# A linear-attention layer and an ELU feed-forward on one core: SP's queue in another order, one block's units three steps apart, and w_out read dense at the end

## The chip, the cores and the metric

One core of one Trainium2 chip. The metric is the device time of one execution in microseconds (us), the median of three runs. The names of the engines are those of the profile: PE is TensorE, DVE VectorE, ACT ScalarE, POOL GpSimd, SP the engine that issues most DMAs.

## The reference

```
# r, k, v: [4, 8, 768, 48]; w, u: [8, 48]; w_in: [384, 2048]; w_out: [2048, 384]
for t in range(768):
    y[t]  = r[t] @ (state + (u * k[t]) outer v[t])       # per batch and head
    state = w * state + k[t] outer v[t]
x = y as [3072 tokens, 8 * 48 channels]
h = x @ w_in
g = where(h > 0, h, exp(min(h, 0)) - 1)
out = g @ w_out                                          # [3072, 384]
```

## The kernel before

**Tiling.** Time is cut into six blocks n of 128 tokens. A block has four **units** (n, b), one for each batch b. A unit computes scores (r by k, decayed), masks them, multiplies them by v, adds what the state gives, and so yields the block's x for its batch; it also adds to the state. A block's x has 4 x 128 = 512 tokens, and the feed-forward runs over it in 16 **steps** f, one for each 128 columns of w_in. The running number of a step is 16 n + f: block 1 starts at step 16, block 2 at 32, block 3 at 48.

**A step.** `hidden` (L1031) writes `ps_h` with nine matmuls: w and x are each split in a high and a low part, and three of the four products are taken for each of three chunks of channels. ACT and DVE make the ELU of it (`negative`, `elu`) and split it in two parts (`split_g`, L1052 and L1054). `project` (L1074) multiplies the split parts of an earlier step by w_out and adds them up in `ps_acc`. Its lag is one step below (n, f) = (1, 4), that is step 20, and two steps from there (`EARLY`). `ps_h` has two buffers. Half of a unit's output, `ps_y`, takes one of them in turn with the steps.

**The last block** (n = 5) is projected by tokens: g is the stationary operand, w_out the moving one, 384 columns wide. w_out lies in the SBUF with its columns permuted (`grouped`, L585), since the other blocks need its columns as rows in that order. So `project` reads it there through `rearrange`, in runs of 32 columns.

**Units from block 2 on.** Their operands are turned through DRAM: DVE transposes r and k in 32 x 32 blocks into `tb` (`t`, `turn_blocks`, L619), SP sends four `blocks` DMAs to DRAM and one back, `rk` (`m`, `move_blocks`, L628 and L633; the latter waits until the four have landed), and POOL multiplies by the powers of w (`br`, `bk`, `decay_moved`, L651). The second of those writes its result back to the buffer of `tb`, and the score matmuls (L758) wait for it. PE's part of a unit stands in `insertion` (`AY`): scores of the new unit, interleaved with the state's part (L766) of the output of the unit before, then that unit's products by v (L791) and the addition to its state (L915).

**x's gap.** A head has 48 channels and 64 rows, so the fourth chunk of an x tile is folded into the free rows of the other three. `G` (`fill_x`, L950) does this with six small DMAs `x<-x` from SP, once the unit's x is split (`xh` on ACT, L940; `xl` on DVE, L942). The first `ps_h` of a block needs the gaps of all its four units.

**What sets the order.** Every engine works in program order, SP's DMA queue too: an issue that waits holds all behind it. The program order is written by hand in two lists of names, `FIRST` for the steps of block 0 and `LATER` for the others. `step` goes through the list once in each step. A name with a letter and a number (`tA-3`, `GY+0`) concerns the unit whose score step (`A`, table `SCORES`) or output step (`Y`, table `OUTPUTS`) is that far from now; a name with a single digit concerns block 1's units in block 0. `rk` and `v` load the raw tensors of a later unit into the slot that this one leaves. There are three slots; the third lies in the tile that held w's raw words (`third_slot`). `ru`, `kr`, `sw`, `p`, `D`, `E` and `sum` are elementwise work of a unit; a `d` behind a name puts it on DVE.

`SCORES` before is 16, 19, 22, 26, 29, 33, 37 and on by fours to 73. Blocks 2 to 5 have four units each, so scores stand at steps 16, 19, 22, 26 (block 2), 29, 33, 37, 41 (block 3), 45 to 57 (block 4), 61 to 73 (block 5). A unit's output is computed in the step of the next unit's scores.

Of the kernel before, what the change touches and what calls it, by code (L numbers as in the profile page):

```python
# [17 lines left out]
P = 128  # L18
B, H, S, D = 4, 8, 768, 48
DP = 64  # L20
HP = H // 2
DM, DFF = 384, 2048
NC = DM // P
# [25 lines left out]


FIRST = """
Eq1 brA-1 rud0 hid ns3 A1 T0 ma sum0 neg mb elu dk0 Y2 xh2 pb1 rk3 tA-3 xl2 sumA-1 sp G2 proj mA-3 gh Lw
Dp0 pa1 lb dr0 r3 gl krd0 swd1 v3 bkA-1 ruA-2 wd r4d third
"""
LATER = """
hid tA-3 AY brA-1 bkA-1 proj neg elu gh gl st nsY+0 xhY+0 xlY+0 paA+1 EqA+1 krA+1 mA-3 rudA-2 pbA+2 swA+2
sumA-1 rkY+0 vY+0 GY+0 DpA+0 out
"""
SCORES = [16, 19, 22, 26] + [13 + 4 * j for j in range(4, 16)]
OUTPUTS = SCORES[1:] + [77]  # L60


class Kernel:
# [319 lines left out]
    def units_at(self, times, step):  # L383
        return [divmod(2 * B + j, B) for j, t in enumerate(times) if t == step]
# [13 lines left out]
    def step(self, n, f):  # L398
        nc = self.nc
# [24 lines left out]
            "Y": lambda n, b: self.outputs(n, b),  # L424
            "xh": lambda n, b: self.split_x(n, b, 0),
            "xl": lambda n, b: self.split_x(n, b, 1),
            "G": lambda n, b: self.fill_x(n, b),
        }
        by_pe = {
            "T": lambda n, b: self.turn_in(n, b),  # L430
# [25 lines left out]
            "lb": lambda: self.low_bits(k + 1),  # L456
            "st": lambda: self.store(last[0]) if last[1] == NF - 1 and last[0] in self.acc else None,
            "out": lambda: self.store_next(),
            "third": lambda: self.third_slot() if (n, f) == (0, 13) else None,
            "AY": lambda: self.insertion(now),  # L460
        }
        now = n * NF + f
        for op in (LATER if n else FIRST).split():
# [3 lines left out]
            if op[-2] in "+-":  # L467
                name, times = op[:-3], (SCORES if op[-3] == "A" else OUTPUTS)
                for m, b in self.units_at(times, now - int(op[-2:])):
# [268 lines left out]
    def insertion(self, now):  # L738

        new, old = (self.units_at(t, now) for t in (SCORES, OUTPUTS))  # L740
        if not new:
# [315 lines left out]
    def project(self, n, f):  # L1057
        gh, gl = self.g.pop((n, f))[2:]
        wh, wl = self.weight(f + 1, 0)
        by_tokens = n + 1 == NCH  # L1060
        if f == 0:
            tags = [(f"acc{c}", 1) for c in range(NC)] + [("rw", 3)] * by_tokens
            self.acc[n] = [
                self.ps.tile([P, 512], F32, tag=tag, name=f"ps_acc{i}", bufs=bufs)
                for i, (tag, bufs) in enumerate(tags)
            ]
        for j, acc in enumerate(self.acc[n]):
            for i, (a, w) in enumerate(((gh, wh), (gh, wl), (gl, wh))):
                if by_tokens:
                    at, lhs = acc[:, 0:DM], a[:, j * P : (j + 1) * P]  # L1070
                    rhs = w.rearrange("p (c i d) -> p i c d", c=NC, i=4)
                else:
                    at, lhs, rhs = acc, w[:, j * P : (j + 1) * P], a
                self.nc.tensor.matmul(  # L1074
                    at, lhsT=lhs, rhs=rhs,
                    start=(f == 0 and i == 0), stop=(f == NF - 1 and i == 2),
                )

    def store(self, n):
        nc = self.nc  # L1080
        acc = self.acc.pop(n)
        if n + 1 == NCH:
            moves = []
            for b, po in enumerate(acc):
                o = self.o.rearrange("p (b d) -> p b d", b=B)[:, b]
                if b % 2:
                    nc.vector.tensor_copy(o, po[:, 0:DM])
                else:
                    nc.scalar.copy(o, po[:, 0:DM])
                row = b * S + n * P  # L1090

                moves.append((self.out[row : row + P, :], o))
                if b != 1:
                    for dst, src in moves:
                        nc.scalar.dma_start(dst, src)
                    moves = []
            return
        o = self.o.rearrange("p (j c d) -> p c j d", j=T // 32, c=NC)
        for c in range(NC):
            nc.vector.transpose(o[:, c], acc[c].rearrange("p (j t) -> p j t", t=32))  # L1100
        self.to_store = [(n, b, i) for b in range(B) for i in range(0, 4, 2)]
        while self.general and self.to_store:
            self.store_next()
# [53 lines left out]
```

## Time and profile before

| | |
|---|---|
| time, median of 3 runs | 530.59 us (529.19 to 530.78) |
| the profiled execution | 528.9 us, its span 527.0 us |
| mean granted TensorE clock | 0.982 |
| PE busy | 503.5 us, 96% |
| DVE, ACT, POOL busy | 59%, 48%, 24% |
| DMA | 50.93 MB, mean 97 GB/s |

The profile is of one execution. Its times count from the start of the span. "Idle before" a row is the time that the engine stood still ahead of it, and the name behind it is what ended that. The granted clock is given as a share of the full 2.4 GHz.

### The profile page before, as it was taken

How to read it: one execution, taken by the hardware profiler on the slowest of the kernel's cores; microseconds unless marked ns; L12 is line 12 of the kernel's file. 1: busy time of each engine (PE TensorE's matmuls, PEld its weight loads, DVE VectorE, ACT ScalarE, POOL GpSimd, SP SyncE). 2: the span in 40 equal slices, each digit the busy share in tenths (PEclk: the TensorE clock that was granted, in tenths of full speed). 3: DMA queues.
4: the chain of work that ended last, by engine and by line, in shares of the span. 5: the costliest groups of instructions: out<-in, count | busy, mean ns of one | idle time of the engine just before them, and what ended most of it. 6: DMA issues, size and time to landing. Idle time of an engine off the chain costs nothing.

```text
span 527.0 us, 9428 instructions
## 1 busy us (share of the span) xinstructions
PE 503.5 (96%) x3584; PEld 416.8 (79%) x3584; DVE 309.1 (59%) x527; ACT 253.5 (48%) x479; POOL 124.6 (24%) x154
## 2 busy tenths in 40 slices
PE   8989999996999999989999989999998999999995
PEld 6987787774878888868888868888786887799995
DVE  5899999983665575645555654654663533433332
ACT  2268788751554345434454453454453543444442
POOL 6832323343231341221311311311202200000000
PEclk9999999997999999999999998999998999999999
DMA  9995869747174444245333344343341200010001
GB/s 136 203 190 136 184 154 232 138 108 155 46 150 108 129 82 107 53 111 124 75 99 94 79 124 90 99 108 77 87 114 38 84 11 8 2 31 24 7 1 65
DMA packets 114203, 50.93 MB, mean 97 GB/s; under 512 B 91362, under 2 KB 110052, under 8 KB 114148
## 3 DMA queue, kind: packets, MB, share of 16 engines
q1 hardware_dynamic: 102052, 45.51, 39.1%
q10 hardware_dynamic: 12096, 4.72, 3.6%
q8 instruction: 30, 0.49, 0.4%
q14 instruction: 25, 0.20, 0.1%
HBM read 35.13 MB, written 13.11 MB: 92 GB/s over the span
## 4 chain that ended last, share of the span: by engine, by line
PE 60%; issue 13%; DMA 8%; DVE 6%; POOL 5%; ACT 4%; SPq 4%; DVEq 0%; POOLq 0%; ACTq 0%
PE ps_acc L1074 25%; PE ps_h L1031 23%; PE ps_y L791 4%; PE ps_a L758 3%; DMA stage<-in_moe_w_in_dram 3%; SPq L950 2%; DMA out_dram<-stage 2%; POOL tb L651 2%; DVE ps_h L1046 1%; PE ps_y L766 1%; PE ps_y L846 1%; ACT g L1041 1%; ACT g L1040 1%; DVE wide L556 1%; POOL a L810 1%
## 5 line engine op out<-in xcount | busy, mean ns | idle before, releaser
L1031 PE MATMUL ps_h<-x,wh 128*128 128x512 f32 (+1 forms) x588 | 181.7, 391 | 4.6 <-DMA x<-x 4.6
L1074 PE MATMUL ps_acc<-g,wh 128*128 128x512 f32 x480 | 166.8, 401 | 0.0
L1046 DVE SCALAR_TENSOR_TENSOR ps_h<-g,ps_h 128x512 f32<-128x512 f32 x96 | 66.6, 694 | 129.3 <-ACT g L1041 129.1
L1031 PEld LDWEIGHTS ps_h<-x,wh 128*128 128x128 f32 x588 | 110.1, 189 | 28.6 <-DMA x<-x 5.0
L1040 ACT ACTIVATE g<-ps_h 128x512 f32<-128x512 f32 x96 | 57.2, 596 | 133.2 <-PE ps_h L1031 121.7
L1031 PE MATMUL ps_h<-x,wl 128*128 128x512 f32 (+1 forms) x294 | 114.4, 389 | 0.0
L1074 PEld LDWEIGHTS ps_acc<-g,wh 128*128 128x128 f32 x480 | 90.6, 189 | 22.0 <-issue 0.9
L1054 DVE TENSOR_TENSOR g<-ps_h,g 128x512 fp32r<-128x512 f32 x96 | 66.3, 691 | 54.2 <-ACT g L1052 52.2
L1074 PE MATMUL ps_acc<-g,wl 128*128 128x512 f32 x240 | 94.3, 393 | 0.0
L1052 ACT CAST g<-ps_h 128x512 fp32r<-128x512 f32 x96 | 56.3, 587 | 65.9 <-DVE ps_h L1046 65.3
L1031 PEld LDWEIGHTS ps_h<-x,wl 128*128 128x128 f32 x294 | 55.7, 189 | 12.0
L1041 ACT ACTIVATE g<-g 128x512 f32<-128x512 f32 x96 | 60.7, 632 | 3.0
L651 POOL TENSOR_TENSOR stage<-rk,pw 128x512 f32<-128x512 f32 x16 | 19.0, 1186 | 170.4 <-DMA rk<-blocks 160.9
L1074 PEld LDWEIGHTS ps_acc<-g,wl 128*128 128x128 f32 x240 | 45.5, 190 | 9.0
L1074 PE MATMUL ps_acc<-wh,g 128*128 128x384 f32 x128 | 35.3, 339 | 0.0
L810 POOL TENSOR_TENSOR a<-ident,diag 128x512 f32<-128x512 f32 x20 | 20.9, 1043 | 56.8 <-PE ps_y L791 53.5
L758 PE MATMUL ps_a<-stage,tb 48*64 48x128 f32 x512 | 26.0, 284 | 7.3 <-POOL tb L651 6.3
L758 PEld LDWEIGHTS ps_a<-stage,tb 48*64 48x64 f32 x512 | 21.5, 139 | 14.0 <-POOL tb L651 10.4
L940 ACT CAST x<-ps_y 128x256 fp32r<-128x256 f32 x40 | 13.1, 377 | 33.6 <-DVE state L930 21.1
L817 DVE COPY_PREDICATED a<-mask,ps_a 128x512 f32<-128x512 int32 x40 | 28.9, 730 | 0.0
L806 ACT ACTIVATE a<-ident,diag 128x128 f32<-128x128 f32 x80 | 25.6, 396 | 0.0
L1074 PEld LDWEIGHTS ps_acc<-wh,g 128*128 128x128 f32 x128 | 23.4, 188 | 1.1 <-issue 0.4
(127 smaller groups left out, 513.6 us busy)
## 6 DMA issues: line engine op xcount, KB each, us to landing
blocks<-tb SPq DMA_DIRECT2D x64, 128.0 KB, 2.3
rk<-blocks SPq DMA_DIRECT2D x16, 512.0 KB, 3.5
stage<-in_moe_w_out_dram SPq DMA_DIRECT2D x16, 384.0 KB, 5.0
stage<-in_moe_w_in_dram SPq DMA_DIRECT2D x32, 144.0 KB, 4.3
out_dram<-stage ACTq DMA_DIRECT2D x80, 48.0 KB, 1.7
r_t<-in_r_dram SPq DMA_DIRECT2D x17, 192.0 KB, 4.3
k_t<-in_k_dram SPq DMA_DIRECT2D x17, 192.0 KB, 4.2
v_t<-in_v_dram SPq DMA_DIRECT2D x17, 192.0 KB, 3.7
```

The source lines that it names most:

```text
L651: self.nc.gpsimd.tensor_mul(dst, src, by)
L758: nc.tensor.matmul(un["pa"][i][keys, a * P : (a + 1) * P], lhsT=un["k"][rows, a, keys], rhs=un["r"][rows, a, :], start=True, stop=True, sk ...
L806: self.nc.scalar.activation(un["a"][i][:, a, :], self.ident, AF.Copy, scale=diag[:, a : a + 1])
L810: self.nc.gpsimd.tensor_mul(un["a"][i], self.ident.unsqueeze(1).to_broadcast([P, HP, P]), diag.unsqueeze(2).to_broadcast([P, HP, P]),)
L817: self.nc.vector.copy_predicated(un["a"][i], self.mask.bitcast(I32).unsqueeze(1).to_broadcast([P, HP, P]), un["pa"][i].rearrange("p (a t) ...
L1031: self.nc.tensor.matmul(ph[:, part], lhsT=a[:, c * P : (c + 1) * P], rhs=x[:, c, part], start=(c == 0 and i == 0), stop=(c == NC - 1 and i ...
L1040: nc.scalar.activation(g, ph, AF.Relu, scale=-1.0)
L1041: nc.scalar.activation(g, g, AF.Exp, scale=-1.0)
L1046: self.nc.vector.scalar_tensor_tensor(ph, g, -1.0, ph, op0=ALU.add, op1=ALU.max)
L1052: nc.scalar.copy(part, g)
L1054: nc.vector.tensor_sub(part, g, self.g[n, f][2].bitcast(F32))
L1074: self.nc.tensor.matmul(at, lhsT=lhs, rhs=rhs, start=(f == 0 and i == 0), stop=(f == NF - 1 and i == 2),)
```

## The change

```
-Eq1 brA-1 rud0 hid ns3 A1 T0 ma sum0 neg mb elu dk0 Y2 xh2 pb1 rk3 tA-3 xl2 sumA-1 sp G2 proj mA-3 gh Lw
-Dp0 pa1 lb dr0 r3 gl krd0 swd1 v3 bkA-1 ruA-2 wd r4d third
+Eq1 rud0 hid ns3 A1 T0 ma sum0 neg mb elu dk0 Y2 xh2 pb1 rk3 xl2 tA-3 sp G2 proj mA-3 gh Lw
+Dp0 pa1 lb dr0 r3 gl krd0 swd1 v3 rudA-2 wd r4d third

-hid tA-3 AY brA-1 bkA-1 proj neg elu gh gl st nsY+0 xhY+0 xlY+0 paA+1 EqA+1 krA+1 mA-3 rudA-2 pbA+2 swA+2
-sumA-1 rkY+0 vY+0 GY+0 DpA+0 out
+hid AY tA-3 brA-1 bkA-1 proj neg elu gh gl st nsY+0 xhY+0 xlY+0 paA+1 EqA+1 krA+1 pbA+2 mA-3 rudA-2 swA+2
+sumA-1 rkY+0 vY+0 GlY+0 GY+1 DpA+0 out

-SCORES = [16, 19, 22, 26] + [13 + 4 * j for j in range(4, 16)]
+SCORES = [17, 20, 23, 26] + [13 + 4 * j for j in range(4, 16)]

-            "G": lambda n, b: self.fill_x(n, b),
+            "G": lambda n, b: self.fill_x(n, b) if n == 1 or b < B - 1 else None,
+            "Gl": lambda n, b: self.fill_x(n, b) if b == B - 1 else None,

-            "third": lambda: self.third_slot() if (n, f) == (0, 13) else None,
+            "third": lambda: self.third_slot() if (n, f) == (0, 14) else None,

 # project, last block
-                    at, lhs = acc[:, 0:DM], a[:, j * P : (j + 1) * P]
-                    rhs = w.rearrange("p (c i d) -> p i c d", c=NC, i=4)
+                    at, lhs, rhs = acc[:, 0:DM], a[:, j * P : (j + 1) * P], w

 # store, last block
-                if b % 2:
-                    nc.vector.tensor_copy(o, po[:, 0:DM])
-                else:
-                    nc.scalar.copy(o, po[:, 0:DM])
+                po = po[:, 0:DM].rearrange("p (c i d) -> p i c d", c=NC, i=4)
+                (nc.vector.tensor_copy if b % 2 else nc.scalar.copy)(
+                    o.rearrange("p (i c d) -> p i c d", c=NC, i=4), po
+                )
```

In `store`, the copies that empty the last block's sums now read the PSUM in the order i, c, d and write their tile in one run. Everything from L428 on stands one line lower in the changed kernel, up to `project`.

The first three units of block 2 have their scores at steps 17, 20 and 23; with them move their transposes, DMAs and elementwise work, the loads of the third slot (one step later), and the outputs, since `OUTPUTS` is made of `SCORES`. The gap of a block's first three units is issued one step later, behind the `blocks` and the `rk` of a unit that comes two later; a block's last unit keeps its place (`Gl`).

**SP's queue around the end of block 0.** `blocks` and `rk` are those of unit (2, 0), `stage` the third slot, `x<-x` the gap of unit (1, 3). Before:

```order
L169 DMA v_t_70<-in_v_dram 128x8x48
L628 DMA blocks<-tb 32x4x256 x4
L633 DMA rk<-blocks 128x1024
L165 DMA stage<-in_r_dram 128x8x48
L165 DMA stage<-in_k_dram 128x8x48
L169 DMA stage<-in_v_dram 128x8x48
L950 DMA x<-x 16x2x128 x6
```

Now:

```order
L169 DMA v_t_70<-in_v_dram 128x8x48
L951 DMA x<-x 16x2x128 x6
L629 DMA blocks<-tb 32x4x256 x4
L634 DMA rk<-blocks 128x1024
L165 DMA stage<-in_r_dram 128x8x48
L165 DMA stage<-in_k_dram 128x8x48
L169 DMA stage<-in_v_dram 128x8x48
```

The gap has passed from behind the blocks, their return and the third slot's three loads to ahead of them.

**SP's queue in steps 33 and 34.** The loads and the gap belong to the unit whose output is computed at step 33, `blocks` and `rk` to the unit whose scores stand at step 37. Before:

```order
L165 DMA stage<-in_r_dram 128x8x48
L165 DMA stage<-in_k_dram 128x8x48
L169 DMA stage<-in_v_dram 128x8x48
L950 DMA x<-x 16x2x128 x6
L628 DMA blocks<-tb 32x4x256 x4
L633 DMA rk<-blocks 128x1024
```

Now:

```order
L165 DMA stage<-in_r_dram 128x8x48
L165 DMA stage<-in_k_dram 128x8x48
L169 DMA stage<-in_v_dram 128x8x48
L629 DMA blocks<-tb 32x4x256 x4
L634 DMA rk<-blocks 128x1024
L951 DMA x<-x 16x2x128 x6
```

The four blocks and their return stand ahead of the gap. The same holds at steps 49 and 65, and for the other units of a block but its last.

**PE behind the first insertion that has an output.** Before, at step 19, where `ps_acc` follows:

```order
L791 MATMUL ps_y<-a,v_t_70 64x128 x8
L915 MATMUL ps_y<-v_t_70,k_t_69 48x48 x8
L1074 MATMUL ps_acc_1581<-g_1637,wh_133 128x512
L1074 MATMUL ps_acc_1581<-g_1637,wl_134 128x512
L1074 MATMUL ps_acc_1581<-g_1639,wh_133 128x512
```

Now, at step 20, where `ps_h` of the next step follows:

```order
L792 MATMUL ps_y<-a,v_t_70 64x128 x8
L916 MATMUL ps_y<-v_t_70,k_t_69 48x48 x8
L1032 MATMUL ps_h<-x,wh_137 128x512 x2
L1032 MATMUL ps_h<-x,wl_138 128x512
L1032 MATMUL ps_h<-x,wh_137 128x512 x2
```

The insertion has moved into the step that has no `project`.

## Rows read from the trace of the kernel before

**Rows 1.** The page: PE's and its weight loads' busy time with the other engines' (section 1), and the granted clock in 40 slices of 13.2 us, in tenths (section 2).

```profile
PE 503.5 (96%) x3584; PEld 416.8 (79%) x3584; DVE 309.1 (59%) x527; ACT 253.5 (48%) x479; POOL 124.6 (24%) x154
...
PEclk9999999997999999999999998999998999999999
```

**Rows 2.** The waits of PE: line and tile, what ended the wait, us in total, times, longest us.

```profile
PE ps_a L758 <- POOL tb L651: 6.3, 6, 2.2
PE ps_h L1031 <- DMA x<-x: 4.6, 1, 4.6
```

**Rows 3.** PE's timeline: start us, duration us, engine, line, operation, output and inputs, count, and in brackets the idle time before and what ended it. The rows with long idle time outside the start, and the insertion of step 19 with the `ps_acc` behind it.

```profile
110.88 1.09 PE L791 MATMUL ps_y<-a,v_t 128*64 128x128 f32 x16 [0.49 <-DVE a L817]
...
123.31 1.19 PE L1031 MATMUL ps_h<-x,wh 128*128 128x512 f32 x2 [4.58 <-DMA x<-x]
...
141.90 0.33 PE L758 MATMUL ps_a<-stage,tb 48*64 48x128 f32 x2
...
144.75 0.50 PE L1074 MATMUL ps_acc<-g,wh 128*128 128x512 f32 x1
...
157.03 0.55 PE L758 MATMUL ps_a<-stage,tb 48*64 48x128 f32 x10 [0.90 <-DVE a L817]
...
233.35 0.33 PE L758 MATMUL ps_a<-stage,tb 48*64 48x128 f32 x2 [2.15 <-POOL tb L651]
...
315.70 0.33 PE L758 MATMUL ps_a<-stage,tb 48*64 48x128 f32 x2 [1.96 <-POOL tb L651]
...
397.62 0.33 PE L758 MATMUL ps_a<-stage,tb 48*64 48x128 f32 x2 [1.64 <-POOL tb L651]
```

**Rows 4.** Windows: the stretch, its length, busy us (and count) of PE, PE's weight loads, DVE, ACT and POOL, the granted clock, the DMA share, GB/s. Directly behind the 4.58 us, and 1.7 us behind the end of the 2.15 us.

```profile
123.30:125.30 2.00, 1.99 (x5) 1.63 (x6) 0.00 (x0) 0.00 (x0) 0.02 (x1) 0.50 0.68 134
...
235.00:237.40 2.40, 2.40 (x33) 2.31 (x31) 0.00 (x0) 0.00 (x0) 0.55 (x1) 0.50 0.02 7
```

**Rows 5.** The chain of waits, pieces in order of time: start us, us, what. Steps 16 and 17, step 33, step 37.

```profile
123.31 4.18 PE ps_h L1031 x9
127.50 1.83 PE ps_a L758 x32
...
131.60 2.08 PE ps_h L1031 x9
...
211.52 0.33 PE ps_a L758 x2
...
212.19 0.44 PE ps_a L758 x16
...
216.73 2.05 PE ps_h L1031 x9
...
233.35 0.33 PE ps_a L758 x2
...
240.13 2.08 PE ps_h L1031 x9
```

**Rows 6.** SP's timeline (columns as in rows 3): the gap and the blocks for step 37, the blocks for steps 53 and 69.

```profile
219.36 3.78 SPq L950 DMA_DIRECT2D x<-x  x6
223.23 1.97 SPq L628 DMA_DIRECT2D blocks<-tb  x4
...
305.75 1.97 SPq L628 DMA_DIRECT2D blocks<-tb  x4
...
386.78 1.98 SPq L628 DMA_DIRECT2D blocks<-tb  x4
```

**Rows 7.** DVE's timeline: the last transposes ahead of those blocks.

```profile
219.87 0.67 DVE L619 STREAM_TRANSPOSE tb<-k_t 128x512 f32<-128x512 f32 x1
...
301.76 1.30 DVE L619 STREAM_TRANSPOSE tb<-stage 128x512 f32<-128x512 f32 x2
...
383.42 0.67 DVE L619 STREAM_TRANSPOSE tb<-k_t 128x512 f32<-128x512 f32 x1
```

**Rows 8.** SP's timeline in steps 13 to 16: unit (2, 0)'s blocks and return, the gap of unit (1, 3).

```profile
110.24 1.77 SPq L628 DMA_DIRECT2D blocks<-tb  x4
115.39 0.34 SPq L633 DMA_DIRECT2D rk<-blocks  x1
...
118.66 4.03 SPq L950 DMA_DIRECT2D x<-x  x6
```

**Rows 9.** DVE's timeline: the split of unit (1, 3)'s x, the ELU of step 15, and the last use of `ps_h` at step 19.

```profile
113.70 0.75 DVE L942 TENSOR_TENSOR x<-ps_y,x 128x256 fp32r<-128x256 f32 x2
...
118.00 0.70 DVE L1046 SCALAR_TENSOR_TENSOR ps_h<-g,ps_h 128x512 f32<-128x512 f32 x1 [2.24 <-ACT g L1041]
...
144.72 0.69 DVE L1054 TENSOR_TENSOR g<-ps_h,g 128x512 fp32r<-128x512 f32 x1 [0.65 <-ACT g L1052]
```

**Rows 10.** POOL's timeline: the product that ends unit (2, 0)'s round trip.

```profile
120.11 1.26 POOL L651 TENSOR_TENSOR tb<-rk,qw 128x512 f32<-128x512 f32 x1
```

**Rows 11.** DMA issues by target and source: queue, count, KB each, median us from issue to landing. The third slot's loads of r.

```profile
stage<-in_r_dram SPq DMA_DIRECT2D x5, 192.0 KB, 4.1
```

**Rows 12.** The chain of waits near the end: nine matmuls of 512 columns (block 4) and twelve of 384 (block 5).

```profile
456.19 2.08 PE ps_acc L1074 x9
...
464.83 2.10 PE ps_acc L1074 x12
```

## The prediction

> **What bounds the kernel now.** I read the page first: PE is busy 503.5 us of a 527.0 us span and the granted clock is full in nearly every slice [rows 1]. So what can be won is PE's idle time and the slow clock behind it, and little else. The waits of PE, taken by themselves, name two large causes: the score matmuls waiting for POOL's `tb`, 6.3 us in six waits, and one `ps_h` matmul waiting 4.6 us for the DMA `x<-x` [rows 2]. PE's timeline gives the places [rows 3]: 2.15, 1.96 and 1.64 us at 233, 316 and 398 us, which are the scores of steps 37, 53 and 69, the second score step of blocks 3, 4 and 5; 4.58 us at 123 us, the first `ps_h` of block 1 (step 16); 0.90 us at 157 us (step 22); 0.49 us at 111 us (step 14). The windows show what follows a long one: PE had run without a gap, stood for about 2 us, and some 1.7 us after it resumed the granted clock is 0.50, the 1.2 GHz level; after the 4.58 us it is 0.50 at once [rows 4]. The chain of waits prices that [rows 5]. From the first score matmul of a unit to the next `ps_h` it takes 5.21 us at step 33 (211.52 to 216.73) and 6.78 us at step 37 (233.35 to 240.13): the slow clock costs 1.57 us more. After the 4.58 us, nine `ps_h` matmuls take 4.18 instead of 2.08 us and 32 score matmuls 1.83 us, where 16 take 0.44 at the full clock: 2.10 + 0.95 = 3.05 us.
>
> Why is `tb` late at steps 37, 53 and 69? SP's queue shows it: six issues of x's gap take 3.8 us, and only then do the next unit's four `blocks` leave, at 223.23, 305.75 and 386.78 [rows 6]. The transposes that feed those blocks had ended 2.69 us earlier each time, at 220.54, 303.06 and 384.09 [rows 7]. From a unit's first block to its scores the round trip is 10.12, 9.95 and 10.84 us (233.35, 315.70, 397.62 less the three starts). In those steps DVE first turns the finished block's sums, so x is split late, the gap waits for it at the head of SP's queue, and the blocks wait behind.
>
> **The change part by part.** *x's gap behind the next unit's blocks.* For a block's second unit the four blocks and `rk` now stand ahead of the gap, so they leave 2.69 us earlier, when the transposes end. That is more than each wait: 0.54, 0.73 and 1.05 us are left over. What goes: 2.15 + 1.96 + 1.64 = 5.75 us idle and 3 x 1.57 = 4.71 us of slow clock, **10.46 us**. The gap now lands some 5 us later; nothing reads it before the next block's first `ps_h`, several steps on, and for a block's last unit, where that is near, it stays ahead. If one of the three waits stayed, 3.5 us of this would be lost.
>
> *The handover to block 1 (steps 13 to 17).* Before, SP issues unit (2,0)'s blocks at 110.24, its `rk` at 115.39, then three loads for the third slot, and only at 118.66 the gap of unit (1,3), for which PE waits [rows 8]. The gap's input was ready when DVE had split it, at 114.45 [rows 9]. Now the gap goes first. The two transposes (1.3 us) also leave DVE's queue ahead of the last score mask and of the split, so the 0.49 us goes and the split ends near 113.35. The six issues take 4.03 us, to 117.4, and PE resumed 0.62 us after the last one (122.69 to 123.31), so x is there at 118.05. PE, which ran dry at 123.31 - 4.58 = 118.73, now does so at 118.24. The wait of step 16 goes, and its slow clock with it.
>
> But unit (2,0)'s blocks now leave at 117.4, not 110.24. Its own round trip was 11.13 us (110.24 to the end of `tb` at 120.11 + 1.26) [rows 10], so its scores can start at 128.5. They are due one step later than before, at 118.24 + 2.08 (`ps_h`) + 2.08 (`ps_acc`) + 2.08 (`ps_h`) = 124.5. **What is late next is therefore this unit**: about 4.0 us idle at step 17. With the shortest trip, 9.95, it is 2.85 us. The slow clock behind it lies between 1.57 us (after about 2 us) and 3.05 us (after 4.58 us); I take 3.05, as 4.0 is nearer to 4.58.
>
> The three loads of the third slot move with it, behind `rk`, to about 123; a load lands 4.1 us after its issue [rows 11], at 127.3, before the transposes of (2,1) at 128.5, which wait for POOL anyway. Two products of (2,0) pass from POOL to DVE (1.1 us) and fall into DVE's idle 2.24 us before 118.00 [rows 9]. I cost both at nothing. If the loads were 2 us later, the transposes and the ELU behind them would be late, but the hidden block's product is not needed until some 6 us after the scores.
>
> *Block 2 three steps apart.* The scores move from steps 16, 19, 22 to 17, 20, 23. Step 20 is the one in which no `ps_acc` is issued (the lag grows from one step to two there). Before, two `ps_h` stood side by side there, DVE fell behind by a step's work, and the mask that the scores of step 22 need came 0.90 us late; now the scores of step 20 stand between the two, and I let the 0.90 us go. But `ps_h` of step 21 follows those scores directly. It needs the `ps_h` buffer that DVE has yet to read. At step 19 DVE ended that read 3.5 us after the scores began (141.90 to 144.72 + 0.69) and PE's insertion took 2.85 us (to 144.75) [rows 3, 9]: a new wait of 0.6 us; between nothing, if DVE is early, and 0.9.
>
> Handover and block 2 together: gone 4.58 + 3.05 + 0.49 + 0.90 = 9.02 us; new 4.0 + 3.05 + 0.6 = 7.65 us; **1.4 us gained**. At the short trip and the small clock cost it would be 9.02 - 2.85 - 1.57 - 0.6 = 4.0; with a trip 1 us longer than (2,0)'s own, 0.3.
>
> *Dense w_out.* The 192 matmuls of the last block read w in one run instead of runs of 32. In the chain twelve of 384 columns take 2.10 us, 175 ns each; nine of 512 dense columns take 2.08, 231 ns each, and three quarters of that is 173 [rows 12]. So runs of 32 cost at most 1.7 ns: 192 x 1.7 = **0.3 us**. The last copy reads PSUM in runs of 32 instead; I put that at nothing, at most 0.3 us, which would cancel the gain. The Trainium skill ("TensorE: Matmul & The Clock Gate", section "Wait — 56ns, not 53.3ns?") has back-to-back matmuls start N / 2.4 GHz + about 2.5 ns apart, 162.5 ns for 384 columns; by that the reordered read would cost 12.5 ns each, 2.4 us in all, and the sum would be 2.1 us lower. The dense rows of this trace stand at 231 ns, where the page would have 215.7, so the excess is not the read order's.
>
> Sum: 10.46 + 1.4 + 0.3 = 12.2 us. The profiled execution took 528.9 us, so 516.7. The three runs before lie at 529.19 to 530.78, median 530.59, all above it; I forecast the new median at **517.5 us**.
>
> **The rivals.** *The handover pays nothing or loses* (0.15). If DVE does not split x earlier (114.45 stays), the gap lands at 119.1, PE waits 0.4 us at step 16, the blocks leave 1.1 us later and step 17 idles some 5 us with the full slow clock: 1.4 turns into about -1.5. For it: ACT's part of the split waits for PE too. Against: DVE's queue loses the 1.3 us. Time 520.5.
>
> *The gap now flies beside `rk`* (0.12). Issued right behind `rk`, its six transfers share the engines with it, and the 0.54 to 1.05 us are used up. Waits of 0.5 to 1 us at two or three places would return 1.5 to 3 us, without a slow clock (after the 0.90 us at 157 us the slices of [rows 1] stay full). Against: the gap moves 16 KB an issue. Time 519.5.
>
> *The round trip is bound by transfers, and the kernel gets slower* (0.05). Blocks sent at once meet the finished block's output stores, which ACT issues in those very steps. With a trip c the four places idle c - 10.6, c - 10.6, c - 11.9 and c - 7.1; together with the new 0.6 us this equals what goes (5.75 + 4.58 + 0.90 + 0.49 + 0.3) at c = 12.9, from which it decides. At c = 14 it is 3.4 + 3.4 + 2.1 + 6.9 us, slow clock as before, 4.4 us slower: 533. For it: 10.84 and 11.13 are above the other two. Against: no trip in the trace reaches 11.2. The Trainium skill ("DMA: Bandwidth & Descriptors", section "Issuing engines are not separate DMA queues") says that transfers of all issuing engines run on the same 16 DMA engines and interleave; by that rule the trips should lengthen, and the trace shows a spread of 1.2 us at most.
>
> *Dense reads are worth 12.5 ns* (0.06): another 2.1 us, 515.4.
>
> That the change doesn't do what it says, the order of the issues excludes for the places that I count; only a block's last unit keeps its gap in front, and no large wait stands there.
>
> **How the numbers follow.** My forecast has 0.62. The range 512.5 to 522.5 takes in the other three cases that are faster and the far ends of the handover (4.0 and 0.3) and of one wait that stays; it leaves out the slow case and mishaps of several kinds. No change means within 0.3%, 1.6 us, about what a measurement of this kernel can tell. Faster 0.93: all cases but the slow one and a little of others; same 0.02; slower 0.05.
>
> **What would show it.** Right: PE's timeline has no wait over 0.5 us at the scores of steps 37, 53 and 69, and the clock stays at 1.00 behind them; in SP's queue `blocks` start as the transposes end, with trips of 10 to 11 us; step 16 starts without a wait; one wait of 2.8 to 4 us for `tb` at step 17, with 0.50 behind it; about 0.6 us before `ps_h` of step 21; twelve `ps_acc` in 2.08 us at the end. Wrong: trips over 12 us, a wait for `x<-x`, or `ps_acc` of the last block under 170 ns.

## The result, and the profile after

The changed kernel takes **516.42 us**, the median of four runs (515.16 to 517.58), where the kernel before took 529.89 us (528.90 to 530.78) beside it: a ratio of 0.9746, 95% interval 0.9714 to 0.9777, or 11.8 to 15.2 us less. The forecast was 517.5 us in a range of 512.5 to 522.5. The profiled execution is the one of 517.58 us, the longest of the four; the profiled one of before, 528.9 us, was its shortest.

The page of the changed kernel, first its span, then the rows that answer to [rows 1]:

```profile
span 515.8 us, 9426 instructions
...
PE 498.1 (97%) x3584; PEld 412.5 (80%) x3584; DVE 316.7 (61%) x529; ACT 253.5 (49%) x479; POOL 125.0 (24%) x152
...
PEclk9999999999899999999999999999999999999999
```

PE is busy 5.4 us less for the same 3584 matmuls. Less of its time runs at the low clock: where [rows 1] has three lower slices, one is left. DVE is busy 7.6 us more. Its products of `ru` alone take 31.8 us where they took 22.2; two of the 40 have moved to DVE (1.1 us), and the rest is that eleven of them take 1.08 to 1.54 us instead of 0.55 (before, two took 0.76 and 1.53). e8 is about that.

The waits of PE, as [rows 2]: line and tile, what ended the wait, us in total, times, longest.

```profile
PE ps_a L759 <- POOL tb L652: 3.8, 3, 3.0
PE ps_a L733 <- DVE rk L664: 3.6, 4, 1.5
...
PE ps_h L1032 <- DVE g L1055: 1.0, 1, 1.0
PE ps_a L759 <- DVE a L818: 0.8, 2, 0.5
```

And its timeline, as [rows 3], the idle time from step 13 on where it is over 0.25 us:

```profile
106.41 1.16 PE L733 MATMUL ps_a<-rk 48*128 48x128 f32 x16 [1.54 <-DVE rk L664]
...
129.60 1.60 PE L759 MATMUL ps_a<-stage,tb 48*64 48x128 f32 x32 [3.03 <-POOL tb L652]
...
149.41 0.73 PE L1032 MATMUL ps_h<-x,wh 128*128 128x512 f32 x2 [1.01 <-DVE g L1055]
...
192.35 0.54 PE L759 MATMUL ps_a<-stage,tb 48*64 48x128 f32 x10 [0.54 <-DVE a L818]
...
290.56 0.33 PE L759 MATMUL ps_a<-stage,tb 48*64 48x128 f32 x2 [0.51 <-POOL tb L652]
...
369.41 0.33 PE L759 MATMUL ps_a<-stage,tb 48*64 48x128 f32 x2 [0.30 <-POOL tb L652]
```

Nothing stands at the scores of steps 37, 53 and 69, nothing at step 16 and nothing at step 23 (the mask that was late at step 22). What is left: 1.54 us for DVE's `rk` at step 13 (no such wait before; the last paragraph of the account comes back to it), 3.03 us at step 17, 1.01 us at the `ps_h` of step 21, 0.54 us at step 29 (new), 0.51 and 0.30 us at steps 49 and 65 (0.20 us each before).

SP's timeline, as [rows 6, 8]: the handover first, then the blocks for steps 37, 53 and 69.

```profile
115.65 3.80 SPq L951 DMA_DIRECT2D x<-x  x6
119.54 1.97 SPq L629 DMA_DIRECT2D blocks<-tb  x4
...
220.58 1.78 SPq L629 DMA_DIRECT2D blocks<-tb  x4
...
299.62 1.79 SPq L629 DMA_DIRECT2D blocks<-tb  x4
...
376.90 1.78 SPq L629 DMA_DIRECT2D blocks<-tb  x4
```

DVE's timeline, as [rows 7, 9]: x's split of unit (1, 3), the last transpose for step 37, and two products of step 27.

```profile
114.88 0.75 DVE L943 TENSOR_TENSOR x<-ps_y,x 128x256 fp32r<-128x256 f32 x2
...
186.63 1.51 DVE L695 TENSOR_TENSOR ru<-stage,u_b 128x384 f32<-128x384 f32 x1
188.18 1.53 DVE L696 TENSOR_TENSOR ru<-ru,stage 128x384 f32<-128x384 f32 x1
...
219.88 0.67 DVE L620 STREAM_TRANSPOSE tb<-k_t 128x512 f32<-128x512 f32 x1
```

POOL's, as [rows 10]: the end of unit (2, 0)'s trip, and what it does beside DVE's two products.

```profile
128.28 1.26 POOL L652 TENSOR_TENSOR tb<-rk,qw 128x512 f32<-128x512 f32 x1
...
186.54 1.19 POOL L652 TENSOR_TENSOR stage<-rk,pw 128x512 f32<-128x512 f32 x1 [6.39 <-DMA rk<-blocks]
187.68 1.61 POOL L652 TENSOR_TENSOR tb<-rk,qw 128x512 f32<-128x512 f32 x1
```

The blocks for step 37 leave at 220.58, 0.03 us after the transposes that end at 220.55. From first block to the end of `tb` the trips at steps 37, 53 and 69 take 10.0, 10.4 and 11.0 us. The handover's gap goes out at 115.65, as DVE's split ends (115.63), and the blocks of (2, 0) at 119.54; their trip ends at 129.54, after 10.0 us.

The chain of waits, as [rows 5, 12]: what follows the 3.03 us, and one projection of the last block.

```profile
129.60 1.60 PE ps_a L759 x32
131.21 3.34 PE ps_acc L1074 x9
134.54 2.08 PE ps_h L1032 x9
...
454.36 2.09 PE ps_acc L1074 x12
```

To compare kernels by stage I take the time from the first `ps_h` of one step to that of a later one, from PE's timeline of each profiled execution (us):

| steps | before | changed | e1 gap | e2 handover | e3 dense | e4 junk |
|---|---|---|---|---|---|---|
| 13 to 24 (handover, block 2) | 63.86 | 62.36 | 64.32 | 60.08 | 64.77 | 65.12 |
| 36 to 39 (scores of 37) | 19.30 | 15.50 | 15.50 | 17.73 | 19.30 | 17.72 |
| 52 to 55 (scores of 53) | 19.04 | 15.46 | 15.46 | 17.73 | 20.90 | 17.87 |
| 68 to 71 (scores of 69) | 18.38 | 15.14 | 15.15 | 18.32 | 16.75 | 16.49 |
| 81 to 95 (last block) | 58.78 | 58.46 | 58.79 | 58.79 | 58.46 | 58.77 |

Between the two executions profiled first, the three stretches of the gap give 3.80 + 3.58 + 3.24 = 10.62 us and the last block 0.3; steps 13 to 24 give 1.50, and steps 24 to 36, which the change also touches (step 29), cost 0.79. The row of steps 13 to 24 has to be read with step 13 in mind: the executions of the changed kernel and of e4 have a wait of about 1.5 us there, the other four of the table under 0.4 us.

### The profile page after: what moved, and what is told of

Same layout as the page of the kernel before. It is cut to its first block, busy times and chain, and to the rows that moved or that the text cites. A ratio compares the mean times of both kernels' runs of the same rounds, so it can differ in the third digit from the quotient of the medians.

```text
span 515.8 us, 9426 instructions
## 1 busy us (share of the span) xinstructions
PE 498.1 (97%) x3584; PEld 412.5 (80%) x3584; DVE 316.7 (61%) x529; ACT 253.5 (49%) x479; POOL 125.0 (24%) x152
## 4 chain that ended last, share of the span: by engine, by line
PE 71%; DVE 8%; issue 6%; DMA 5%; ACT 5%; POOL 3%; SPq 1%; DVEq 0%; ACTq 0%; POOLq 0%
PE ps_acc L1074 31%; PE ps_h L1032 29%; DMA stage<-in_moe_w_in_dram 5%; PE ps_y L792 3%; PE ps_a L759 3%; DVE ps_h L1047 2%; DVE wide L557 1%; ACT stage L549 1%; PE ps_y L767 1%; DVE wide L565 1%; PE ps_y L847 1%; ACT stage L543 1%; PE ps_y L916 1%; ACT g L1041 1%; POOL tb L652 1%
## 5 line engine op out<-in xcount | busy, mean ns | idle before, releaser
L1032 PEld LDWEIGHTS ps_h<-x,wl 128*128 128x128 f32 x294 | 55.2, 188 | 11.9
```

The source lines that it names most:

```text
L1032: self.nc.tensor.matmul(ph[:, part], lhsT=a[:, c * P : (c + 1) * P], rhs=x[:, c, part], start=(c == 0 and i == 0), stop=(c == NC - 1 and i ...
```

## The experiments

e1 to e3 are the kernel before with one part of the change each, and e4 is the kernel before with a few matmuls added. e5 to e8 alter one thing in the changed kernel, c1 to c4 build on e8. Ratios are to the kernel before, run beside them; differences in us from the kernel before are worked out from the ratio, those from the changed kernel are differences of medians.

**e1: the gap alone.** The kernel before with

```
-sumA-1 rkY+0 vY+0 GY+0 DpA+0 out
+sumA-1 rkY+0 vY+0 GlY+0 GY+1 DpA+0 out
```

and the two entries for `G` and `Gl`.

> The kernel before with x's gap behind the next unit's blocks for a block's first three units, and nothing else of the change. My theory: the waits of 2.15, 1.96 and 1.64 us at the scores of steps 37, 53 and 69 go and the clock stays full behind them, 10.46 us in all, so 10.5 us below the kernel before; the 4.58 us at step 16 and the 0.90 us at step 22 stay. Rival (the gap flies beside rk): waits of 0.5 to 1 us stay at two or three of these places, 7.5 to 9 us gained. Rival (the three waits cost only their idle time, and the slow clock behind them would come anyway): 5.75 us gained.

Measured: 519.6 us, ratio 0.9827 (0.9779 to 0.9875), 9.2 us less (6.6 to 11.7). In the trace the three waits are gone (the table: 15.50, 15.46 and 15.15 us, those of the whole change) and the handover is the old one. PE's timeline, the first `ps_h` of block 1, and the only other wait for `tb` over 0.3 us:

```profile
124.34 1.19 PE L1032 MATMUL ps_h<-x,wh 128*128 128x512 f32 x2 [4.57 <-DMA x<-x]
...
292.44 0.33 PE L759 MATMUL ps_a<-stage,tb 48*64 48x128 f32 x2 [0.75 <-POOL tb L652]
```

The mechanism is shown. The gap flying beside `rk` used no margin up, so that rival falls, and the 5.75 us of the other lie outside the interval. Whether the slow clock was priced rightly, e2 and e4 tell.

**e2: the handover and block 2 alone.** The new `FIRST`, `tA-3` behind `AY`, `pbA+2` ahead of `mA-3`, the new `SCORES`, the third slot at (0, 14); `GY+0` and the reads of w_out as before.

> The kernel before with the new order of steps 12 to 15, block 2's scores at steps 17, 20 and 23 and the third slot one step later; the gap keeps its place behind later units' outputs, w_out is read as before. My theory, by the prediction's terms: 1.4 us gained. By what the changed kernel's trace shows of the terms (3.03 us idle at step 17 with about 1.7 us of slow clock, 1.01 and 0.23 us at steps 21 and 20, against 9.02 us that go): about 3 us gained. Rival (the handover loses): 1.5 us slower. The waits at steps 37, 53 and 69 stay, about 2 us each.

Measured: 525.65 us, ratio 0.9911 (0.9872 to 0.9950), 4.7 us less (2.6 to 6.8). The part that I had put at 1.4 us is worth more. PE's timeline, the scores of steps 17 and 37:

```profile
128.04 1.10 PE L758 MATMUL ps_a<-stage,tb 48*64 48x128 f32 x32 [3.04 <-POOL tb L651]
...
229.76 0.33 PE L758 MATMUL ps_a<-stage,tb 48*64 48x128 f32 x2 [2.15 <-POOL tb L651]
```

The wait at step 37 is 2.15 us, as in [rows 3]. But the chain shows the products by v and the `ps_acc` behind it at the full clock, and those behind the 1.60 us of step 69 at the low one:

```profile
231.31 1.02 PE ps_y L791 x16
232.69 2.30 PE ps_acc L1074 x9
...
392.98 1.90 PE ps_y L791 x16
394.88 2.82 PE ps_acc L1074 x9
```

Behind the same 2.15 us the kernel before had a granted clock of 0.50 [rows 4]; here the window behind it has 1.00:

```profile
231.50:233.90 2.40, 2.40 (x38) 2.11 (x35) 0.71 (x2) 0.24 (x1) 1.45 (x2) 1.00 0.03 8
```

The stretch takes 17.73 us in place of 19.30: 1.57 less, with the wait still there. Step 53 repeats it (2.15 us of wait, 17.73 us). Steps 13 to 24 take 3.78 us less than before in this execution.

**e3: w_out read dense, alone.** `rhs` is `w` in the last block, and the last copies permute.

> The kernel before with the last block's w_out read in one run of 384 columns, and the permuted copies at the end. My theory: 0.3 us gained, at most 0.4 (a step of the last block takes 4.155 us instead of 4.18 in the changed kernel's chain, sixteen times), which the runs can hardly tell from nothing. Rival (reads in runs of 32 cost 12.5 ns a matmul): 2.4 us gained.

Measured: 530.37 us, ratio 1.0004 (0.9974 to 1.0034), between 1.4 us less and 1.8 us more. The runs exclude 2.4 us and can't see 0.3. The trace can: steps 81 to 95 take 58.46 us where all kernels with the old read take 58.77 to 58.79, so 0.32 us for fourteen steps and 0.37 for sixteen, 1.9 ns a matmul.

**e4: the slow clock behind the three waits.** The kernel before with

```
+        for _ in range(6 if now in (37, 53, 69) else 0):
+            nc.tensor.matmul(un["pa"][0][:, 0:P], lhsT=self.ident, rhs=self.ident, start=True, stop=True)
```

in `insertion`.

> The kernel before with six more 128 x 128 matmuls (about 0.235 us each, 1.41 us in all, their result is overwritten) on PE ahead of the scores of steps 37, 53 and 69. They fill part of the 2.15, 1.96 and 1.64 us that PE waits for tb, and end no wait. My theory: PE goes on in these places at the full clock, the 3 x 1.57 us behind the waits go, 4.7 us below the kernel before, while the scores start at the same distance from their blocks; idle of about 0.7, 0.5 and 0.2 us is left. Rival (the slow stretch has another cause than the idle PE): no gain, the clock still 0.50 behind the scores. Second rival (the junk is in the way): up to 1 us slower.

Measured: 527.38 us, ratio 0.9965 (0.9929 to 1.0002), 1.9 us less (3.8 less to 0.1 more). PE's timeline and the chain behind it:

```profile
235.81 0.33 PE L762 MATMUL ps_a<-stage,tb 48*64 48x128 f32 x2 [0.79 <-POOL tb L651]
```

```profile
237.36 1.02 PE ps_y L795 x16
238.74 2.30 PE ps_acc L1078 x9
```

In the profiled executions the three stretches are 1.58, 1.17 and 1.89 us shorter than before, 4.64 together, as the theory had it. The runs give under half of that, and their interval leaves 4.7 out. The theory's price holds where the low clock comes, but it does not come behind every such wait in every execution: e2 shows that at step 37, and so does e3 at step 69, with 1.53 us of wait and 16.75 us for the stretch, where the kernel before had 1.64 us [rows 3] and 18.38. The clocks of the runs agree. 29 runs of the kernel before had a mean granted clock of 0.978 to 0.993. Span x (1 - clock), an estimate of what the low clock costs a run, is 3.7 to 11.7 us there, 8.0 on average; in the ten runs of e4 it is 5.3. That is 2.6 us for the three places, not 4.7.

The second rival, that the junk is in the way, is not excluded by this. In e4's profiled execution steps 39 to 52 take 64.97 us where the kernel before had 63.25, with waits of 0.92 and 0.87 us for `tb` at steps 45 and 49, and no run tells whether the extra matmuls had a part in that. The estimate from the clock does not depend on it.

**e5: the step without `ps_acc` one later.** The changed kernel with `EARLY = (1, 5)`.

> The changed kernel with EARLY = (1, 5) in place of (1, 4): the step without ps_acc is 21 instead of 20, so nine ps_acc (2.08 us) stand between the insertion of step 20 and the ps_h of step 21. My theory (that ps_h waits because it follows the insertion directly): the 1.01 us at step 21 goes, no wait over 0.3 us takes its place, 1.0 us gained on the changed kernel's 516.42. Rival (the wait is the gap between DVE's work and PE's over the whole stretch, and moves with it): a wait of about 1 us appears at the next place, the scores or the ps_h of step 23, and the time is the same.

Measured: 518.64 us, ratio 0.9776 (0.9711 to 0.9841). The 1.01 us is gone, and PE's timeline has this at step 23:

```profile
160.64 0.55 PE L759 MATMUL ps_a<-stage,tb 48*64 48x128 f32 x10 [2.03 <-DVE a L818]
```

The rival holds in its mechanism: DVE is behind over the whole stretch, and the wait moves to where its work is next needed. It does not hold in size, since 2.03 us are twice what went; c2 takes that apart. The median is 2.2 us above the changed kernel's, with overlapping intervals, and the profiled execution lost more to the clock behind the 2.85 us at its step 17. The chain there:

```profile
127.93 1.98 PE ps_a L759 x32
129.92 4.14 PE ps_acc L1074 x9
```

**e6: the slow clock at step 17.** The same extra matmuls as in e4, `11 if now == 17 else 0`, in the changed kernel.

> The changed kernel with eleven more 128 x 128 matmuls (0.235 us each, 2.6 us in all, their result is overwritten) on PE ahead of the scores of step 17, in the 3.03 us that PE waits for tb. My theory: about 0.4 us of idle time is left, the clock stays full behind it, nine ps_h take 2.08 instead of 3.34 us and the 32 score matmuls under 1.2 instead of 1.60 us: 1.7 us gained in an execution that had the slow clock there. Rival (no slow clock is saved, or the junk pushes the scores later in executions whose wait is shorter): no change.

Measured: 514.68 us (514.46 to 515.64), ratio 0.9713 (0.9666 to 0.9760). The expected 1.7 us below the changed kernel's median; the two intervals overlap, so the size rests on the trace and the clock. PE's timeline:

```profile
127.86 1.10 PE L763 MATMUL ps_a<-stage,tb 48*64 48x128 f32 x32 [0.58 <-POOL tb L652]
```

And the chain behind it:

```profile
128.96 2.28 PE ps_acc L1078 x9
```

The 32 score matmuls take 1.10 instead of 1.60 us and the nine `ps_acc` behind them 2.28 instead of 3.34, so the low clock behind the 3.03 us had cost 0.50 + 1.06 = 1.56 us. The mean clock of the four runs is 0.998, of the changed kernel's 0.995. The expectation named `ps_h` where `ps_acc` stands.

**e7: the last unit's gap behind the blocks too.** `GY+1` for all four units in the changed kernel.

> The changed kernel with the gap of a block's last unit behind the next blocks too (GY+1 for all four units). My theory: the 0.51 and 0.30 us at the scores of steps 49 and 65 go, and no wait for x<-x appears at the first ps_h of steps 32, 48, 64 and 80, since the last unit's output is computed three steps ahead: 0.8 us gained. Rival (that gap is needed soon, which its own place in the change would suggest): waits for x<-x at two or more of those steps, slower.

Measured: 520.61 us, ratio 0.9804 (0.9751 to 0.9858). The rival holds: PE waits 1.41, 2.25 and 1.14 us for `x<-x` at the first `ps_h` of steps 32, 48 and 64. The longest of the three, and SP's timeline ahead of step 32:

```profile
286.90 0.70 PE L1031 MATMUL ps_h<-x,wh 128*128 128x512 f32 x2 [2.25 <-DMA x<-x]
```

```profile
197.64 1.77 SPq L628 DMA_DIRECT2D blocks<-tb  x4
201.31 0.34 SPq L633 DMA_DIRECT2D rk<-blocks  x1
201.75 3.79 SPq L950 DMA_DIRECT2D x<-x  x6
```

`rk` holds the queue from 199.4 until the blocks have landed, and only then do six issues follow, to 205.54; PE needed x at 204.55 (205.96 less 1.41). Behind the blocks and `rk`, the gap starts 4.1 us after the first block (201.75 less 197.64). Here that is too late.

**e8: DVE's products away from POOL's.** In the changed kernel `rudA-2` stands behind `AY` instead of behind `mA-3`, so the two products of `ru` come ahead of that step's ELU.

> The changed kernel with the two products of ru (two steps ahead of a unit's scores) at the start of that step's work on DVE, ahead of the ELU, where DVE stands idle 2.85 us at 181.20, instead of at its end, where they run beside POOL's two products. My theory (DVE's and POOL's products slow each other): every ru product takes 0.55 to 0.56 us where the changed kernel's took up to 1.55, the 0.54 us at step 29 and the 0.23 us at step 20 go, and part of the 1.01 us at step 21: 0.8 to 1.3 us gained. Rival (the long ones are something else, as data that is still landing): they stay at 1.5 us and the waits stay.

Measured: 514.90 us, ratio 0.9723 (0.9673 to 0.9773), 1.5 us below the changed kernel's median, again with overlapping intervals. DVE's timeline, the products of step 27:

```profile
177.35 0.55 DVE L695 TENSOR_TENSOR ru<-stage,u_b 128x384 f32<-128x384 f32 x1
177.94 0.56 DVE L696 TENSOR_TENSOR ru<-ru,stage 128x384 f32<-128x384 f32 x1
```

The same two products took 1.51 and 1.53 us beside POOL's in the changed kernel, so the theory holds and the rival falls. All means of `ru`'s groups on DVE are 547 to 559 ns now, the 0.54 us at step 29 and the 0.23 us at step 20 are gone, and the wait at step 21 is 0.65 instead of 1.01 us. Steps 24 to 36 take 58.83 us, where the changed kernel had 59.83 and the kernel before 59.04.

Moving the products also takes 1.1 us of work from that place in DVE's order, so e8 alone does not show that their slowness made the waits. Other executions do, with the products in the old place. Ahead of the scores of step 20 they took 1.08 and 1.54 us in the changed kernel and 0.94 and 1.53 in e7, and PE waits 1.01 us at step 21 in both. In e2 and e6 they end as POOL starts or before, and take 0.54 and 0.56 us; there step 20 waits for nothing, and step 21 waits 0.66 us. Ahead of the scores of step 29 it is the same: 0.54 us of waiting behind products of 1.51 and 1.53 us, 0.30 behind 1.26 and 1.53 (e6), and none behind 1.10 and 0.76 (e2).

**c1: the handover's gap from two queues.** e8, and of unit (1, 3)'s gap the half i = 1 is issued by `nc.scalar` behind `gh` (a `Ga2` in `FIRST`).

> The changed kernel with ru early (as in e8_ru_early, 514.9 us) and with three of the six issues of unit (1, 3)'s gap on ACT's queue, behind split_g, where ACT stands idle 3.13 us ahead of the ELU at 116.23. My theory (the 2.75 us at step 17 are unit (2, 0)'s round trip, which starts only when SP has issued the gap): the blocks of (2, 0) start about 1.9 us earlier, 0.8 us of the wait is left and no slow clock behind it, 1.9 us gained on e8_ru_early and up to 1.7 us more where it had the slow clock: about 512 to 513. Rival (the trip gets longer by as much, as loads and gap share the DMA engines): the wait stays over 2 us. Second rival (ACT's issues hold its ELU, and PE waits for ps_h or g at steps 16 and 17): no gain.

Measured: 513.19 us, ratio 0.9684 (0.9634 to 0.9734). PE's timeline, the scores of steps 17 and 20:

```profile
126.71 1.10 PE L760 MATMUL ps_a<-stage,tb 48*64 48x128 f32 x32 [0.89 <-POOL tb L653]
...
141.96 0.33 PE L760 MATMUL ps_a<-stage,tb 48*64 48x128 f32 x2 [1.49 <-POOL tb L653]
```

SP's timeline:

```profile
114.58 1.89 SPq L952 DMA_DIRECT2D x<-x  x3
116.57 1.97 SPq L630 DMA_DIRECT2D blocks<-tb  x4
...
128.54 3.92 SPq L630 DMA_DIRECT2D blocks<-tb  x4
136.04 0.34 SPq L635 DMA_DIRECT2D rk<-blocks  x1
```

Step 17 is as expected: ACT's three issues (2.18 us) run beside SP's three (1.89), the blocks leave 2.0 us after the gap's first issue instead of 3.9, 0.89 us of wait is left and the clock stays full. But a wait of 1.49 us is new at step 20, and the 16 products by v behind it take 1.58 us where they take 1.02 at the full clock. The blocks of (2, 1) now take 3.92 us to issue, and their trip is 13.4 us (128.54 to 141.90); in e8 the same blocks took 2.07 us and 10.7. They leave 1.5 us after six loads that follow each other without a break, and two of these loads land only after that, at 128.70 and 129.88 us. The windows have the DMA share at 1.43 from 128 to 130 us (a transfer counts whole where it starts, so the share can pass 1); in e8 the last of the six was held up by its slot, and the share was 0.84 when the blocks left (130 to 132 us). c2 and c3 have the same six loads without a break, and the same trip takes 13.5 and 13.4 us there. That the loads cause it fits, but no run took them away. Part of the gain is so given back.

**c2: c1 with the lag at step 21.** `EARLY = (1, 5)` added.

> As c1_two_queues, and the step without ps_acc moved from 20 to 21 (as in e5_lag_step21). In e5 the wait at step 21 went and one of 2.03 us for the mask came at step 23. My theory: part of those 2.03 us came from the slow ru products, which are gone here; the 0.65 us at step 21 goes and under 1.6 us, the kernel before's and e3's range (0.90 to 1.58 us), stands at step 23: 0 to 1 us slower than c1. Rival (the whole 2.03 us was the slow products): no wait over 0.3 us at either place, 0.6 us faster than c1.

Measured: 512.20 us (511.96 to 512.80), ratio 0.9681 (0.9634 to 0.9728). The wait at step 20 is there again (1.72 us). There is none at step 21, and 0.75 us at step 23: of e5's 2.03 us the slow products had made more than half, and what is left is about what e8 had at step 21. c1 itself has no wait at step 21, behind its 1.49 us at step 20, so the time could not fall by the 0.65 us. Against c1 the runs don't tell it apart.

**c3: c1 with two queues for every block's last gap.** `GbY+0` issues the half i = 1 from ACT.

> As c1_two_queues, and half of the gap of a block's last unit on ACT's queue in the later blocks too. In e8_ru_early this gap's six issues took 5.02 us at 271.33 and the blocks for step 49 left behind them, with a wait of 1.04 us at step 49. My theory: those blocks leave about 2 us earlier, the 1.04 us at step 49 and any at step 65 go, 0.5 to 1 us faster than c1. Rival (an issue on ACT's queue waits there for DVE's split and holds ACT's ELU behind it): new waits for g or ps_h at steps 45, 46, 61 and 62, slower than c1.

Measured: 512.19 us (510.42 to 513.37), ratio 0.9685 (0.9636 to 0.9734). Step 20 waits 1.57 us and step 21 0.35. No wait over 0.1 us stands behind step 21 in PE's timeline; steps 49 and 65 are clean, and ACT holds nobody up. The 0.51 and 0.30 us of the changed kernel are not the most that the last unit's gap in front can cost: with it whole, PE waits 1.03 us at step 49 in e5 and 1.04 there in e8, and 1.14 and 1.42 us at step 65 in e6 and c4. In the last two the blocks also landed later: `rk` left 5.5 and 5.8 us after the first block, in the changed kernel 3.9. c3's profiled span of 508.4 us is the shortest of all; by the ratio it equals c1 and c2.

**c4: e8 and e6 together.**

> The changed kernel with ru early (e8_ru_early) and the eleven more matmuls ahead of the scores of step 17 (e6_junk_17) together. If the two effects are separate: the idle time at step 17 under 0.6 us with the clock full behind it, the ru products at 0.55 us, 1.5 us each below the changed kernel's 516.42, about 513.3. If both had only removed the same slow stretch: as e6 or e8 alone, 514.7 to 514.9.

Measured: 513.58 us, ratio 0.9705 (0.9655 to 0.9755), 0.72 us of wait at step 17 with the full clock behind it, the products at 0.55 us. In the trace both effects are there, each as in its own run, so they are separate. The times alone cannot say so: the interval is 2.6 us to either side, and 513.3 and 514.8 us both lie in it.

c1 to c3 are 16.7 to 16.9 us below the kernel before (14.1 to 19.4), against 13.5 for the change (11.8 to 15.2).

## Why the prediction was right, and which terms were off

The time was 1.1 us from the forecast. The parts alone give 9.2 + 4.7 - 0.2 = 13.7 us, the whole 13.5, so they add up, each within some 2 us. That the forecast came so near is in part luck: by the medians the first term was 1.3 us too large and the second 3.3 too small. Term by term:

- **The three waits, 10.46 us.** Right in every step that the trace shows: blocks leave as the transposes end, trips of 10.0 to 11.0 us, the clock full behind the scores, and 10.62 us between the two executions profiled. Probably too large for the median: the 3 x 1.57 us of slow clock were read off one execution in which it came at all three places, and by e4 they are worth about 2 to 3 us in the mean of many. e1 measured 9.2 us for the term, and its interval (6.6 to 11.7) would still hold 10.46. The prediction calls these the second score steps of blocks 3, 4 and 5 and speaks of a block's second unit. By `SCORES` they belong to each block's third unit, and the gap that stood ahead of its blocks is the first unit's; no number depends on that.
- **The handover and block 2, 1.4 us.** This was mis-sized: 4.7 us by e2 (2.6 to 6.8), and 3.78 in steps 13 to 24 of its profiled execution; the far end of the prediction was 4.0. The changed kernel's own profiled execution shows only 1.50 there, with 1.54 us of waiting at step 13 in it, so it agrees with the 1.4 by accident. The idle time at step 17 is 3.03 us, not 4.0, because I took (2, 0)'s old trip of 11.13 us over; the new one takes 10.0, and 2.85 was the value for the shortest trip of before. The slow clock behind it I put at 3.05 us, since 4.0 was nearer to 4.58; it cost 1.56. Together these are 2.5 of the 3.3 us; the rest I can't place, and it is less than the width of e2's interval. The 3.05 us were a little too large where they were read, too: the prediction counts the 32 score matmuls of step 17 at 0.88 us at the full clock, twice 0.44, and e6 has them at 1.10. The split did end earlier in DVE's queue: counted from the first `ps_h` of step 14 (107.55 before, 109.69 now, behind the wait at step 13) after 5.94 us instead of 6.90. `ps_h` of step 16 waited for nothing.
- **The 0.6 us at step 21** came as 1.01, and as 0.65 or 0.66 in e2, e6 and e8, where DVE's products ahead of it aren't slowed. e5 and c2 correct my reason: it isn't only that `ps_h` follows the insertion directly, since with nine `ps_acc` between the two the wait comes at step 23; DVE is behind from step 19 to 23.
- **Not in the sum: DVE against POOL.** I moved a unit's trip earlier and did not ask what POOL's two products, which end it, then run beside. They now meet DVE's products of `ru` at more places (eleven slowed products instead of two), and both waits that come of it (0.54 us at step 29, 0.23 at step 20) are the mask that DVE takes afterwards. e8 took them away. The Trainium skill ("SBUF — State Buffer", section "SBUF: two separate sides") has a DVE operation with two SBUF inputs and a GpSimd operation that reads SBUF take turns on one shared pair of ports, each for its whole instruction. The trace agrees: a product that takes 0.55 us alone took 1.51 beside POOL's, and POOL's second one took 1.61 there where it took 1.26 at 128.28.
- **Dense w_out, 0.3 us.** 0.37 by the trace, and the rival of 2.1 us more is excluded by e3. Twelve `ps_acc` take 2.09 us with dense reads, 174 ns each. The Trainium skill ("TensorE: Matmul & The Clock Gate", section "Wait — 56ns, not 53.3ns?") would have 162.5 ns by the estimate in the prediction; the trace does not agree, and the excess was not the order of the reads.
- **The rivals.** The trips of the three places grew by at most 0.5 us (9.95 to 10.4 at step 53), and the slower case did not come. But c1 to c3 have a trip of 13.4 to 13.5 us, beyond the 12.9 from which that rival decides, at one place: blocks that left right behind six loads. And the trips differ from one execution to the next: the one for step 65 took 11.6 and 11.9 us to its scores in e6 and c4, 10.8 in the changed kernel.

What stays open: in the profiled execution of the changed kernel block 0 ran 0.7 us later up to step 13 and PE waited 1.54 us there for DVE's `rk`, in an order that the change leaves alone; e4, without the change, had 1.52 us at the same place, and the other profiled executions have up to 0.77. No run tells why it differs. Nor does one tell in which executions the low clock comes.

## What to carry to other kernels

In a queue that is worked off in order, put first what starts a round trip, unless what it displaces is due within the length of that trip: the gap of a block's first three units could wait, that of the last could not (e7). A wait's price is its idle time plus what the clock loses behind it, and the second part must be read from several executions, not from the one that was profiled. When a transfer is made earlier, look up what the engine that receives it will then run beside.

## What the runs showed of the hardware

The low clock behind a wait of about 2 us is not fixed. Behind 2.15 us it cost 1.57 us in one execution and nothing in another (e2). Behind about 3 us at step 17 it cost 1.56 us in the changed kernel and 2.77 in e5, where the 32 score matmuls took 1.98 us instead of 1.10, the next nine `ps_acc` 4.14 instead of 2.28 and the nine `ps_h` 2.11 instead of 2.08. In the kernel before it makes an estimated 3.7 to 11.7 us of a run, and the times go with it (correlation 0.89 over the 29 runs). It is not all of the spread: in e4 two runs with a clock of 0.992 took 525.36 and 529.72 us. With a few matmuls whose results are thrown away put into the wait, the clock stayed full behind each of the five waits so filled in the profiled executions (e4, e6, c4). Behind 1.5 to 2.2 us it also stayed full without them at five places (steps 37 and 53 in e2, 69 in e3, 20 in c2 and c3); behind the five unfilled waits of 2.75 to 3.04 us at step 17 (the changed kernel, e2, e5, e7, e8) it fell every time, and the nine `ps_acc` there took 3.31 to 4.14 us.

Three issues each from two queues at the same moment took 1.89 and 2.18 us, where six from one took 3.79. The Trainium skill ("DMA: Bandwidth & Descriptors", section "Issuing engines are not separate DMA queues") says that this saves only the time to issue, usually small beside the transfer; here the time to issue was what the blocks waited for.
